# First head pair's bias tiles on GpSimd's queue, with two steps of the hand-over to attention in another order

## The chip, the cores and the metric

The kernel runs on 1 core of one Trainium2 chip. The metric is device time in microseconds (us), the median of several executions: 493.66 us over 3 runs before the change (493.31 to 494.21).

## The reference

Attention over 4 batches, 8 heads, 576 positions and head size 64, with a learned bias on relative position, and behind it a feed-forward block with a gate. All inputs and outputs are float32.

```python
scores = scale * np.matmul(q, k.transpose(0, 1, 3, 2))          # 4 x 8 x 576 x 576
x = (psi_rel / psi_i)[..., None]                                # log1p|i-j| / log1p(max(i,1))
h = np.maximum(x @ w1 + b1, 0.0)                                # 576 x 576 x 32
bias = h @ w2                                                   # 576 x 576 x 8, the same for every batch
attn = softmax(scores + bias)                                   # row maximum taken off first
x = matmul(attn, v)                                             # to 4 x 576 x 512
h = np.maximum(x @ w_in, 0.0)                                   # 4 x 576 x 1024
conv_out = sum over k of conv_w[k] * h[shifted by k - 1]
out = (h * sigmoid(conv_out)) @ w_out                           # 4 x 576 x 512
```

## The kernel before, in words

The program has three stages. The instructions of each engine run in the order in which the code emits them.

**The bias stage** computes the bias once for all batches. It goes over 36 blocks of 16 query rows (the loop over `i`). For a block, VectorE (DVE) and ScalarE (ACT) make the hidden layer (`y`, lines 246 and 250), TensorE (PE) contracts it with `w2` (line 267), and ACT copies the result from PSUM into one of five staging buffers (`st`, of which one is called `tl`, line 293). Each pair of blocks is then written to a scratch tensor in DRAM, `bias_d`, by one DMA of 607 KB on SyncE's (SP's) queue (line 306). This text calls blocks 2k and 2k+1 pair k, so pair 0 is the first.

**The bias tiles** are read back from `bias_d` by `load_bias(p, t)` (lines 173 to 184), a head pair p and a unit t at a time. The rows of queries are cut into five units: unit 0 has the first 64 rows of both heads on top of each other (one tile of 128 rows), units 1 to 4 have 128 rows each for each of the two heads. Each tile takes two DMAs, one for a head. Pair 0's tiles go through SP's queue, those of the other three head pairs through GpSimd's (POOL's) queue. A tile can be read once the pairs of blocks with its rows have landed in DRAM, and the queue that issues the read waits for that; whatever stands behind it on the same queue waits too. Unit 0's tile needs pairs 0 and 1, unit 1's needs pairs 2 to 5, and so on by four.

**The attention stage** walks over 16 combinations n of head pair and batch, and in each over the units t. For a unit, PE makes the scores (`s`, line 363), DVE adds the bias tile and takes the row extreme in one instruction per head (line 374, "reduce"), ACT takes the exponential with the row sum (line 388, "exponential") and marks the buffer by a two-column write (`sr`, line 342), PE transposes the result (lines 422 and 434), ACT and DVE copy the transposes from PSUM (lines 90 and 93), and PE multiplies them with V (line 471, "PV"). The transposes of line 422 go into free columns of the same PSUM tile as the last head's scores, so that head's reduce follows them. PV of a group (units 0 to 2, or 3 and 4) is cut into five parts, which wait in the queue `fill` and are put between other units' work. POOL stores and spreads the inverse row sums (lines 498 to 504) and applies them to the output (line 511).

Four units of n = 0, that is (0,0) to (0,3), start inside the bias loop, so that the stages overlap: at `i` = 13, 21, 29 and 34. Unit (0,3) has its scores and reduce there, its exponentials later. Behind the loop comes the **hand-over**: the last blocks are written, the tile of unit (0,4) is loaded, the first unit of n = 1 gets its scores, and the rest of `fill` is emitted. The list `flat` then sets the order of all units that are left. The main loop does, in iteration u, the scores and reduces of unit u+2, the exponentials of unit u+1, and the transposes of unit u, followed by parts of PV. `sums` says in which iteration the inverse row sums of the n before are transposed, `invert` (lines 486 and 487) makes them on DVE, and `load` and `load_v` fetch the next q, k and v through SP's queue.

**The feed-forward stage** takes the last 200 us and is not touched.

Of the kernel before, what the change touches and what calls it, by code (L numbers as in the profile page):

```python
# [19 lines left out]
def attention_ffn_kernel(  # L20
# [11 lines left out]
    nc = tc.nc  # L32
# [53 lines left out]
    NSEQ = len(seq)  # L86
# [50 lines left out]
    with tc.manual_schedule():  # L137
# [33 lines left out]
            nc.sync.dma_start(vt[TL:P, 9], v[b, p, TL:P, 4])  # L171

        def load_bias(p, t, cuts=()):
            queue = nc.gpsimd if p else nc.sync
            bt = bias_p.tile([P, 2, S], F32, name="bt") if t else bias0_p.tile([P, 1, S], F32, name="bt0")
            for a, e in zip((0,) + cuts, cuts + (P,)):
                for h in range(2):
                    c = (2 * p + h) * BW
                    if t:
                        i0 = TL + (t - 1) * P  # L180
                        queue.dma_start(bt[a:e, h], bias_rows[i0 + a:i0 + e, c:c + S])
                    else:
                        queue.dma_start(bt[TL * h:TL * h + TL, 0, :], bias_rows[0:TL, c:c + S])
            biast[p, t] = bt
# [155 lines left out]
        def turned_sp(n, t):  # L340
            tile = sp_p.tile([P, 2 * S + 2], F32R, name="sr", tag=spt[n, t][1])
            nc.scalar.activation(tile[:, 2 * S:], pars[:, 0:2], AF.Copy)
            spt[n, t] = (tile, None)


        def scores(n, t, h):
            p, b = seq[n]
            qt = qks[n]
            if h == 0:
                if n not in sms:  # L350
                    sms[n] = sm_p.tile([P, 9], F32, name="sm")
                nms[n, t] = sm_p.tile([P, 2], F32, name="nm")
                new_sp(n, t)
            ps = psum["s"].tile([P, 2, 512], F32, name="s")


            ops = [(h, h * QW + P * t, slice(0, P))] if t else [
                (hh, hh * (QW + TL), slice(TL * hh, TL * hh + TL)) for hh in range(2)
            ]
            for hh, qo, po in ops:  # L360
                for a in range(2):
                    rows = slice(D * a, D * a + D)
                    nc.tensor.matmul(  # L363
                        ps[po, a, 0:HS],
                        qt[rows, qo:qo + po.stop - po.start],
                        qt[rows, KO + hh * HS:KO + hh * HS + HS],
                        start=True,
                        stop=True,
                    )
            return ps  # L370

        def reduce(ps, n, t, h):
            bt = biast[seq[n][0], t]
            nc.vector.tensor_tensor_reduce(  # L374
                out=halves(spt[n, t][0][:, h]),
                in0=ps[:, :, 0:HS],
                in1=halves(bt[:, h]),
                op0=ALU.add,
                op1=ALU.min,
                scale=-scale,  # L380
                scalar=3.0e38,
                accum_out=nms[n, t][:, h:h + 1],
            )

        def expo(n, t, h):
            sp, nm = spt[n, t][0], nms[n, t]
            col = 4 * h + t - 1 if t else 8
            exps[n, t, h] = nc.scalar.activation(  # L388
                sp[:, h], sp[:, h], AF.Exp, bias=nm[:, h:h + 1], scale=-1.0,
                accum_out=sms[n][:, col:col + 1],  # L390
            )
# [187 lines left out]
        first = [(0, 0), (0, 1), (0, 2), (0, 3)]  # L579
        flat = [(n, t) for n in range(1, NSEQ) for t in units]  # L580
        flat.insert(0, (0, 3))
        flat.insert(3, (0, 4))
        NU = len(flat)

        def heads(t):
            return (0, 1) if t else (0,)

        fill = deque()
# [24 lines left out]
        for i in range(NBLK):  # L613
            nxt = bias_hidden(i + 1) if i + 1 < NBLK else None
            bias_mm(i, hidden)
            if last:
                bias_out(*last)
            last = (i,)
            hidden = nxt
            if i % 8 == 6 % 8 and i >= 6:  # L620
                load_bias(0, (i - 6) // 8)
            if i == 2:
                load(0)
            if i == 4:
                load_v(0)
            if i == 16:
                load(1)
            if i == 20:
                load_v(1)
            if i in starts:  # L630
                unit = unit_steps(*first[starts.index(i)])
            if unit:
                next(unit, None)
            for _ in range(max(0, i - starts[-1] + 1)):
                fill.popleft()()
        bias_out(*last)
        load_bias(0, 4, (96,))
        reduce(scores(*flat[1], 0), *flat[1], 0)
        while fill:
            fill.popleft()()  # L640
        early.close()
        psT = pool(ctx, "psT", 3, space=PSUM)
        psO = pool(ctx, "psO", 1, space=PSUM)
        psum.update(s=psS, tp=psT, o=psO)
        for h in heads(flat[0][1]):
            expo(*flat[0], h)
        turned_sp(*flat[0])
        pv_share = (2, 2, 1, 3, 2)
        hs_ff = {}
        raw_w = {}  # L650
# [4 lines left out]
        for u, (n, t) in enumerate(flat):  # L655
            p, b = seq[n]
            ui = units.index(t)
            sums = n - 1 if ui == 2 and n else None
            side = None
            if u + 2 < NU:  # L660
                for h in heads(flat[u + 2][1]):
                    if side is not None:
                        reduce(side, *flat[u + 2], 0)
                    side = scores(*flat[u + 2], h)
            if t:
                if side is None:
                    side = psS.tile([P, 2, 512], F32, name="s")
                side_transposes(side, n, t, sums)
            if u + 2 < NU:
                reduce(side, *flat[u + 2], h)  # L670
            if u + 1 < NU:
                for h in heads(flat[u + 1][1]):
                    expo(*flat[u + 1], h)
                turned_sp(*flat[u + 1])
            transposes(n, t, side, sums)
            next(job_steps, None)

            parts = len(fill) if u < 5 else pv_share[ui]
            while fill and parts > 0:
                fill.popleft()()  # L680
                parts -= 1
            next(job_steps, None)
            del spt[n, t]
            if u + 2 >= NU:
                f = u + 2 - NU
                hs_ff[0, f] = ffn_in(0, f)
            if u == 1 or n and ui == 2 and n + 2 < NSEQ:
                load(2 if u == 1 else n + 2)
            if u in conv_weights:
                conv_weights[u]()  # L690

            for at, do in ((u - 7, "load"), (u - 11, "split")):
                job = at // 2
                if at % 2 == 0 or not 0 <= job < 4 * KC + 2 * FE:
                    continue
                if job < 4 * KC:
                    src, dst = w_in[job // 4 * P:job // 4 * P + P], wi[job // 4]
                else:
                    src, dst = w_out[(job - 4 * KC) // 2 * P:(job - 4 * KC) // 2 * P + P], wo[(job - 4 * KC) // 2]
                cs = slice(job % 4 * 256, job % 4 * 256 + 256) if job < 4 * KC else slice(job % 2 * 256, job % 2 * 256 + 256)  # L700
                if do == "load":
                    raw_w[job] = (e_p if job % 3 else woe_p).tile([P, 256, 2], I32, name="raw_w", tag="h")
                    load_w(raw_w[job], src[:, cs])
                else:
                    job_steps = split_w_steps(e_p, dst[:, :, cs], raw_w.pop(job), ("cv", "cv"))
            if u + 2 < NU:
                n2, t2 = flat[u + 2]
                p2, b2 = seq[n2]
                if b2 == B - 1 and p2 + 1 < NP:
                    load_bias(p2 + 1, t2)  # L710
            if ui == (0 if n > 1 else 1) and n > 0:
                invert(n - 1)
            if ui == (2 if n > 1 else 3) and 1 <= n and n + 1 < NSEQ:
                load_v(n + 1)
            if ui == 3 and n > 0:
                store_sums(n - 1)
            if ui == 4 and n > 0:
                spread_sums(n - 1)
            if ends_group(n, t):
                fill.extend(pv_parts(n, t > 2))  # L720

            if ui == 2 and n > 1:
                apply_norm(n - 2)
            if n == NSEQ - 2 and ui > 1:
                x_parts(0, ui - 2)
            if n == NSEQ - 1 and ui == 0:
                x_parts(0, 3)
            if n == NSEQ - 1 and ui in (1, 2):
                load_wo(FE - 1 + ui)
# [209 lines left out]
```

## Time and profile before

| | |
|---|---|
| median of 3 runs | 493.66 us |
| the profiled execution | 493.83 us |
| its span, first to last instruction | 492.1 us |
| PE busy | 478.5 us (97%) |
| DVE busy | 376.9 us (77%) |
| ACT busy | 311.4 us (63%) |
| POOL busy | 154.0 us (31%) |
| granted TensorE clock | 1.00 throughout |

The span is that of one profiled execution; the difference to its device time, 1.7 us, lies around it. A share over the whole span says little here, since the three stages have different limits. So the rows further down are read by stage: the bias stage runs to about 62 us, the hand-over to about 78 us, attention to about 290 us. Idle time in the rows stands before the instruction that it precedes, with what released it.

### The profile page before, as it was taken

Reading aid. Unit: us, or ns where it says so; the run is one execution under the profiler, and the core shown is the slowest. Engines: PE = TensorE matmul, PEld = TensorE weight load, DVE = VectorE, ACT = ScalarE, POOL = GpSimd, SP = SyncE. Lnnn points to the kernel's source line nnn. Section 1 sums busy time; section 2 is a strip of 40 time slices with the busy share of each in tenths; the row PEclk is TensorE's granted clock in tenths of the full one; section 3 lists DMA queues with packets and bytes.
Section 4 is the critical chain, followed back from the end, with each engine's and each line's share of the span. In section 5 each row is a group of like instructions: output and inputs, shape, how many; then the busy total and the mean of one; then the engine's idle time right before and its main releaser. Section 6 shows DMA issues by size and latency. Waiting matters only on the chain.

```text
span 492.1 us, 11067 instructions
## 1 busy us (share of the span) xinstructions
PE 478.5 (97%) x4202; PEld 353.1 (72%) x4202; DVE 376.9 (77%) x871; ACT 311.4 (63%) x751; POOL 154.0 (31%) x215
## 2 busy tenths in 40 slices
PE   6989999999999999999999999999999999999996
PEld 4333356666666666666666689889988999899986
DVE  6989967788898889988898729944896279838930
ACT  6989877888888889888888736712542144224510
POOL 1000001245455735565547725160081005400000
PEclk9999999999999999999999999999999999999999
DMA  1999667388667895589751300002000300020011
GB/s 38 280 332 318 253 194 172 93 277 214 158 180 201 225 254 157 161 218 290 191 130 50 111 25 26 2 0 87 0 1 0 108 1 1 1 85 1 1 44 64
DMA packets 32584, 60.82 MB, mean 124 GB/s; under 512 B 7196, under 2 KB 15796, under 8 KB 32532
## 3 DMA queue, kind: packets, MB, share of 16 engines
q1 hardware_dynamic: 27380, 47.02, 33.2%
q0 software_dynamic: 4768, 12.77, 8.8%
q8 instruction: 33, 0.54, 0.5%
q10 hardware_dynamic: 384, 0.35, 0.2%
q14 instruction: 19, 0.16, 0.1%
HBM read 44.12 MB, written 15.98 MB: 122 GB/s over the span
## 4 chain that ended last, share of the span: by engine, by line
PE 88%; ACT 5%; DVE 3%; DMA 3%; issue 1%; SPq 0%; DVEq 0%
PE s L536 21%; PE o L471 17%; PE s L363 16%; PE tp L786 16%; PE tp L434 9%; PE o L786 4%; PE s L267 2%; DVE y L250 2%; DMA bias_d<-st 1%; ACT st L293 1%; ACT y L246 1%; ACT sp L388 1%; PE s L422 1%; DVE sp L374 1%; DMA pars<-in_par_dram 1%; DMA bt<-bias_d 1%
## 5 line engine op out<-in xcount | busy, mean ns | idle before, releaser
L374 DVE CUSTOM_DVE_ANT_0 sp<-s,bt 128x576 f32<-128x576 f32 x144 | 104.1, 754 | 32.3 <-PE s L363 13.1
L388 ACT ACTIVATE sp<-sp,nm 128x576 f32<-128x576 f32 x144 | 109.9, 767 | 0.8 <-DVE nm L374 0.8
L536 PEld LDWEIGHTS s<-xs,wi 128*128 128x128 f32 x768 | 102.8, 189 | 1.2 <-issue 0.5
L536 PE MATMUL s<-xs,wi 128*128 128x288 f32 x768 | 103.6, 296 | 0.0
L363 PE MATMUL s<-qk 64*128 64x288 f32 (+1 forms) x640 | 92.6, 431 | 0.5 <-DVE pty L93 0.2
L363 PEld LDWEIGHTS s<-qk 64*128 64x128 f32 (+1 forms) x640 | 46.9, 175 | 42.1 <-DVE nm L374 12.1
L786 PE MATMUL tp<-wo,g 128*128 128x512 f32 x288 | 70.7, 390 | 0.0
L434 PE MATMUL tp<-identr,sr 64*128 64x64 f32 x1184 | 64.3, 247 | 0.0
L786 PEld LDWEIGHTS tp<-wo,g 128*128 128x128 f32 x288 | 53.7, 188 | 11.8 <-DVE g L781 0.9
L434 PEld LDWEIGHTS tp<-identr,sr 64*128 64x128 f32 x1184 | 55.5, 136 | 5.6 <-issue 0.6
L761 DVE SCALAR_TENSOR_TENSOR cv<-h,cw,cv 128x575 f32<-128x575 f32 x64 | 55.2, 863 | 2.5 <-ACT cv L756 0.6
L548 ACT ACTIVATE h<-s 128x576 f32<-128x576 f32 x32 | 20.8, 651 | 55.2 <-PE s L536 55.2
L267 PE MATMUL s<-y,pars 128*32 128x512 f32 (+8 forms) x352 | 46.8, 513 | 4.0 <-DVE y L250 3.4
L250 DVE TENSOR_SCALAR y<-tl,inv,nb 128x576 f32<-128x576 f32 (+33 forms) x112 | 47.6, 506 | 0.1
L471 PE MATMUL o<-ptx,vt 128*64 128x320 f32 x300 | 47.0, 442 | 0.0
L471 PE MATMUL o<-pty,vt 128*64 128x256 f32 x320 | 44.2, 393 | 0.0
L133 POOL TENSOR_SCALAR xs<-x 128x576 fp32r<-128x576 f32 x16 | 15.2, 950 | 81.4 <-PE s L536 66.5
L267 PEld LDWEIGHTS s<-y,pars 128*32 128x32 f32 x352 | 17.3, 115 | 30.6 <-DVE y L250 15.3
L767 ACT ACTIVATE cv<-cv 128x576 f32<-128x576 f32 x32 | 21.8, 680 | 23.6 <-DVE cv L761 23.6
L498 POOL DMA_DIRECT2D r_d<-rt x16 | 10.0, 625 | 82.9 <-DVE rt L93 82.9
L768 DVE SCALAR_TENSOR_TENSOR cv<-cv,h 128x576 f32<-128x576 f32 x32 | 29.6, 924 | 5.7 <-ACT cv L767 5.7
L93 DVE COPY ptx<-tp 128x256 f32<-128x256 f32 (+1 forms) x64 | 32.0, 499 | 1.4 <-PE tp L434 1.2
(83 smaller groups left out, 635.8 us busy)
## 6 DMA issues: line engine op xcount, KB each, us to landing
qk<-in_qk_dram SPq DMA_DIRECT2D x32, 320.0 KB, 5.1
bias_d<-st SPq DMA_DIRECT2D x13, 607.0 KB, 5.0
bt<-bias_d POOLq DMA_DIRECT2D x24, 288.0 KB, 5.5
qk<-in_qk_dram SPq DMA_DIRECT2D x32, 144.0 KB, 5.4
rb<-r_d POOLq DMA_DIRECT2D x32, 144.0 KB, 3.1
vt<-in_v_dram SPq DMA_DIRECT2D x16, 256.0 KB, 5.9
raw_w<-in_moe_w_in_dram SPq DMA_DIRECT2D x16, 256.0 KB, 5.0
out_dram<-o SPq DMA_DIRECT2D x16, 256.0 KB, 2.0
```

The lines of the kernel that those rows point to most:

```text
L93: nc.vector.tensor_copy(o, i)
L250: nc.vector.tensor_scalar(y, dist[:, 0:n], inv[:, ig:ig + 1], nb1, op0=ALU.mult, op1=ALU.max)
L267: nc.tensor.matmul(ps[32 * j:32 * j + 32, a // 512 if n > 512 else blk % 2, 0:min(n - a, 512)], w2b, ys[j][:, a:min(n, a + 512)], start=Tr ...
L363: nc.tensor.matmul(ps[po, a, 0:HS], qt[rows, qo:qo + po.stop - po.start], qt[rows, KO + hh * HS:KO + hh * HS + HS], start=True, stop=True,)
L374: nc.vector.tensor_tensor_reduce(out=halves(spt[n, t][0][:, h]), in0=ps[:, :, 0:HS], in1=halves(bt[:, h]), op0=ALU.add, op1=ALU.min, scale ...
L388: exps[n, t, h] = nc.scalar.activation(sp[:, h], sp[:, h], AF.Exp, bias=nm[:, h:h + 1], scale=-1.0, accum_out=sms[n][:, col:col + 1],)
L434: tr = nc.tensor.transpose(ps[a][:, TL * s:TL * s + TL].bitcast(F32R), spf[ra, j:j + P], identr[ra, ra])
L471: nc.tensor.matmul(po[D * h:D * h + D, 0:width], vt[:, slot, :], pt[:, blk, :], start=(c == 0), stop=(c == 4),)
L536: nc.tensor.matmul(ps[:, a, 0:HS], wi[c][:, pw, cs], xss[b, c][:, px, a * HS:(a + 1) * HS], start=(i == 0), stop=(i == 3 * KC - 1),)
L761: nc.vector.scalar_tensor_tensor(out=cv[:, o:o + S - 1], in0=h[:, i:i + S - 1], scalar=cw[:, f, kk:kk + 1], in1=cv[:, o:o + S - 1], op0=AL ...
L768: nc.vector.scalar_tensor_tensor(out=cv, in0=cv, scalar=1.0, in1=h, op0=ALU.add, op1=ALU.mult)
L786: nc.tensor.matmul(ps, lhs(f, gi), wo[f][:, wj, cs], start=(f == 0 and i == 0), stop=(f == FC - 1 and i == 2),)
```

## The change

Pair 0's tiles for units 0 to 3 move from SP's queue to POOL's, and their loads are emitted two blocks earlier, right behind the last block that they need. Unit (0,4)'s tile stays on SP's queue. The exponentials of unit (0,3) are emitted ahead of the rest of `fill`. Unit (0,4) moves from fourth to fifth place in `flat`, and with it move the iterations for `sums` and `invert` of n = 0, the load of q and k for n = 2, and the place of one group of PV.

```diff
         def load_bias(p, t, cuts=()):
-            queue = nc.gpsimd if p else nc.sync
+            queue = nc.sync if cuts else nc.gpsimd
...
         flat.insert(0, (0, 3))
-        flat.insert(3, (0, 4))
+        flat.insert(4, (0, 4))
...
-            if i % 8 == 6 % 8 and i >= 6:
-                load_bias(0, (i - 6) // 8)
+            if i % 8 == 4:
+                load_bias(0, i // 8)
...
         load_bias(0, 4, (96,))
         reduce(scores(*flat[1], 0), *flat[1], 0)
+        for h in heads(flat[0][1]):
+            expo(*flat[0], h)
+        turned_sp(*flat[0])
         while fill:
             fill.popleft()()
         early.close()
         psT = pool(ctx, "psT", 3, space=PSUM)
         psO = pool(ctx, "psO", 1, space=PSUM)
         psum.update(s=psS, tp=psT, o=psO)
-        for h in heads(flat[0][1]):
-            expo(*flat[0], h)
-        turned_sp(*flat[0])
...
-            sums = n - 1 if ui == 2 and n else None
+            sums = n - 1 if ui == (2 if n > 1 else 3) and n else None
...
+            while fill and u == 5:
+                fill.popleft()()
             transposes(n, t, side, sums)
...
-            if u == 1 or n and ui == 2 and n + 2 < NSEQ:
-                load(2 if u == 1 else n + 2)
+            if u in (2, 4) or n > 1 and ui == 2 and n + 2 < NSEQ:
+                load(n + 2 if n > 1 else 2 + u // 4)
...
-            if ui == (0 if n > 1 else 1) and n > 0:
+            if ui == (0 if n > 1 else 2) and n > 0:
                 invert(n - 1)
```

SP's queue in the bias stage, with the reads of the bias tiles (`bt`) among the writes of the staging buffers; rows with a minus are of before.

```order
 L306 DMA bias_d<-st_125 128x2x607
-L183 DMA bt_266<-bias_d 64x576 x2
 L306 DMA bias_d<-st_132 128x2x607 x2
 L306 DMA bias_d<-tl 128x2x607
 L306 DMA bias_d<-st_124 128x2x607
-L181 DMA bt<-bias_d 128x576 x2
 L306 DMA bias_d<-st_125 128x2x607
```

The reads leave SP's queue here and at two later places. On POOL's queue they stand between its first fills of constants and the first inverse row sums (`r_d`).

```order
 L318 MEMSET rr_155 128x128
 L222 MEMSET kv 128x2
+L183 DMA bt_243<-bias_d 64x576 x2
+L181 DMA bt<-bias_d 128x576 x6
 L498 DMA r_d<-rt 2x4x128
 L499 DMA r_d<-rt 2x1x64
```

Nothing else of POOL stands between the eight reads. ACT at the hand-over, before the change: the last copies of the bias stage (`st`), the copy of an output of PV (`x`), then the exponentials.

```order
L293 ACTIVATE st_125<-s,kv 128x576
L293 ACTIVATE st_125<-s,kv 128x31
L90 ACTIVATE x_121<-tp 128x320
L388 ACTIVATE sp,sm<-sp,nm 128x576 x2
L342 ACTIVATE sr<-pars 128x2
L388 ACTIVATE sp,sm<-sp,nm 128x576
```

And after it.

```order
L293 ACTIVATE st_125<-s,kv 128x576
L293 ACTIVATE st_125<-s,kv 128x31
L388 ACTIVATE sp,sm<-sp,nm 128x576 x2
L342 ACTIVATE sr<-pars 128x2
L90 ACTIVATE x_121<-tp 128x320
L388 ACTIVATE sp,sm<-sp,nm 128x576
```

The two exponentials of unit (0,3) and the write behind them have moved ahead of the copy. PE in iterations 4 to 6 of the main loop, before: scores (L363), transposes (L422, L434), transposes of the inverse row sums (L426) and PV (L471).

```order
L363 MATMUL s<-qk 128x288 x4
L422 MATMUL s<-identr,sr 128x64 x2
L426 MATMUL s<-ident,rr_154 128x64 x2
L434 MATMUL tp<-identr,sr 128x64 x16
L471 MATMUL o<-pty,vt_106 64x256 x10
L363 MATMUL s<-qk 64x288 x4
L422 MATMUL s<-identr,sr 128x64 x2
L434 MATMUL tp<-identr,sr 128x64 x16
L471 MATMUL o<-ptx,vt_107 64x320 x6
L363 MATMUL s<-qk 128x288 x4
L422 MATMUL s<-identr,sr 128x64 x2
L434 MATMUL tp<-identr,sr 128x64 x16
```

And after it.

```order
L363 MATMUL s<-qk 128x288 x4
L422 MATMUL s<-identr,sr 128x64 x2
L434 MATMUL tp<-identr,sr 128x64 x16
L471 MATMUL o<-ptx,vt_107 64x320 x10
L363 MATMUL s<-qk 64x288 x4
L422 MATMUL s<-identr,sr 128x64 x2
L426 MATMUL s<-ident,rr_154 128x64 x2
L471 MATMUL o<-pty,vt_106 64x256 x10
L434 MATMUL tp<-identr,sr 128x64 x16
L363 MATMUL s<-qk 128x288 x4
L422 MATMUL s<-identr,sr 128x64 x2
L434 MATMUL tp<-identr,sr 128x64 x16
```

The wider group of PV (`ptx`, of n = 1) comes first and whole, the other one (`pty`, of n = 0) one iteration later and ahead of that iteration's transposes; the sums move with it.

## Rows read from the trace of the kernel before

**Rows 1.** Busy us by stretch (PE, PEld, DVE, ACT, POOL), granted clock, DMA share, GB/s.
```profile
26.00:62.00 36.00, 33.50 (x270) 12.39 (x270) 33.73 (x84) 31.55 (x59) 0.00 (x0) 1.00 0.87 296
...
78.00:285.00 207.00, 207.00 (x2368) 137.91 (x2365) 174.94 (x498) 169.40 (x472) 109.44 (x168) 1.00 0.68 182
```
**Rows 2.** Chain of waits, bias stage: start us, us, what.
```profile
14.64 7.12 DMA bias_d<-st
...
22.32 3.31 DMA bt<-bias_d
```
**Rows 3.** Timeline of VectorE: start us, us, engine line op, [idle before <-releaser].
```profile
25.80 0.76 DVE L374 CUSTOM_DVE_ANT_0 sp<-s,bt 128x576 f32<-128x576 f32 x1 [0.99 <-PE s L267]
...
44.72 5.71 DVE L250 TENSOR_SCALAR y<-tl,inv,nb 128x436 f32<-128x436 f32 x13
...
66.77 0.76 DVE L374 CUSTOM_DVE_ANT_0 sp<-s,bt 128x576 f32<-128x576 f32 x1 [1.23 <-ACT x L90]
...
68.30 0.76 DVE L374 CUSTOM_DVE_ANT_0 sp<-s,bt 128x576 f32<-128x576 f32 x1 [0.77 <-PE s L422]
```
**Rows 4.** Timeline of TensorE, same columns.
```profile
27.00 1.86 PE L267 MATMUL s<-y,pars 128*32 128x352 f32 x8 [1.48 <-DVE y L250]
...
68.01 0.25 PE L422 MATMUL s<-identr,sr 64*128 64x64 f32 x2 [0.90 <-ACT sp L388]
...
79.78 0.72 PE L363 MATMUL s<-qk 64*64 64x288 f32 x8
```
**Rows 5.** Chain of waits at the hand-over.
```profile
66.45 1.52 ACT sp L388 x4
...
74.07 0.09 DVE rr L486
...
74.19 0.22 DVE rr L487
...
76.05 0.72 PE s L363 x3
...
77.54 2.31 PE o L471 x20
```
**Rows 6.** Timeline of ScalarE, bias stage and hand-over.
```profile
18.06 1.45 ACT L293 ACTIVATE st<-s,kv 128x960 f32<-128x960 f32 x2
...
66.01 0.44 ACT L90 ACTIVATE x<-tp 128x320 f32<-128x320 f32 x1 [2.88 <-PE tp L471]
```
**Rows 7.** Timeline of SyncE's queue: issues of DMAs.
```profile
21.82 1.09 SPq L183 DMA_DIRECT2D bt<-bias_d  x2
23.00 1.05 SPq L306 DMA_DIRECT2D bias_d<-st  x2
...
72.03 0.62 SPq L154 DMA_DIRECT2D qk<-in_qk_dram  x1
```
**Rows 8.** Timeline of GpSimd: its first DMAs.
```profile
79.31 0.54 POOL L499 DMA_DIRECT2D r_d<-rt  x1
84.18 1.07 POOL L504 DMA_DIRECT2D rb<-r_d  x2 [4.33 <-DMA r_d<-rt]
```
**Rows 9.** DMA issues near 79, 84 and 96 us: count, KB each, us to landing.
```profile
r_d<-rt POOLq DMA_DIRECT2D x1, 0.5 KB, 4.3
...
rb<-r_d POOLq DMA_DIRECT2D x2, 144.0 KB, 3.1
...
bt<-bias_d POOLq DMA_DIRECT2D x2, 144.0 KB, 4.9
```
**Rows 10.** Timeline of GpSimd and VectorE, near 105 and 139 us.
```profile
104.67 1.69 POOL L181 DMA_DIRECT2D bt<-bias_d  x3
...
105.96 0.28 DVE L99 TENSOR_SCALAR wu<-raw_w 128x256 int32<-128x256 int32 x1
...
139.16 1.52 POOL L511 TENSOR_TENSOR x<-x,rb 128x576 f32<-128x576 f32 x1
...
139.29 1.53 DVE L99 TENSOR_SCALAR wu<-raw_w 128x256 int32<-128x256 int32 x1
```

## Prediction

> **What bounds the kernel now.** The page was read first, then busy time by stretch, then the chain of waits through the first 82 us, then the timelines of the engines that it passes. From 78 us to 285 us PE is busy in all of its 207.00 us [rows 1]: attention runs at PE's pace, and whatever comes late before 78 us comes late at the end. So the question is how much earlier or later PE gets into its unbroken stretch, which begins with PV at 77.54 [rows 5].
>
> In the bias stage no engine is free to catch up. DVE is busy 33.73 of 36.00 us, PE 33.50, ACT 31.55 [rows 1], and they hand blocks to each other. The chain enters this stage through a transfer: pair 1's write is issued at 14.64 and takes 7.12 us, so it lands at 21.76; the second half of unit 0's tile is issued at 22.32 and lands 3.31 us later, at 25.63 [rows 2]. DVE, which runs in order, has by then been idle 0.99 us ahead of unit 0's reduce at 25.80 [rows 3]; behind it PE waits 1.48 us for the next `y` [rows 4]. The release that the row of DVE names is an older one of PE; the chain shows the tile. I found no wait in the stretch behind it that would take up a further delay: what DVE, PE and ACT do next all hangs on that reduce or on the `y` behind it. So each 1 us by which unit 0's tile is later counts as 1 us at the end.
>
> At the hand-over the chain goes through ACT: it copies PV's output at 66.01 after 2.88 us of idleness [rows 6], and then makes four pieces of exponentials in 1.52 us from 66.45 [rows 5], two for unit (0,3). PE waits 0.90 us for them, up to 68.01 [rows 4], and DVE's second reduce of unit (1,1) follows at 68.30, since its PSUM tile is also written by those transposes [rows 3]. From there DVE has no idle row until PV has begun, and DVE's last copy lets PE go on at 76.05 [rows 5].
>
> **The exponentials.** They need only the reduces of unit (0,3), done while ACT sits idle ahead of 66.01. Two of them with their write fit into those 2.88 us. PE's wait goes, and the reduce at 68.30 can follow the one at 66.77, which takes 0.76 [rows 3]: it starts at 67.53, 0.8 us sooner. That is all that can go there, because the reduce at 66.77 waits for scores that PE makes after PV, in an order that stays. What is late next is DVE, which then runs without a break up to the end of the hand-over, so the 0.8 us arrives whole at PV. ACT is not late: it got rid of 1.52 us and of the write ahead of DVE's stretch.
>
> **The unit put later.** Iterations 0 to 4 hold the same units as before in another order, so PE, ACT and DVE have the same work ahead of PV, with one exception. `invert` took DVE 0.09 + 0.22 = 0.31 us of the chain [rows 5], ahead of the reduces and of the copy that frees PSUM for PE. One iteration later it stands behind the last copy that PE waits for. That is another 0.3 us. The transposes of the sums move behind that point too; they are 0.1 us at most. Behind PV's start the order of PV changes, not its amount, and PE has always something to do: five parts of the wide group, then five of the narrow one, then an iteration without PV, in which DVE and ACT have two iterations of PV as a lead. I cost this at nothing; if the cover failed, an iteration without PV would cost the 0.2 us or so by which a reduce follows PE's scores. The load for n = 2 is issued an iteration later; before, its last issue is at 72.03 [rows 7] and its first use at 79.78 [rows 4], 7.75 us later. One iteration less, some 2 us, leaves more than the 4.9 us that the slowest transfer in rows 9 takes. SP has nothing urgent behind it. POOL's first inverse sums come an iteration later, with DMAs and a multiplication behind them that nobody in attention waits for.
>
> Sum of these two edits: 0.8 + 0.3 = 1.1 us sooner.
>
> **The tiles on POOL's queue.** Eight reads leave SP's queue. What they held up was writes: pairs 3 and 4 were issued from 23.00 [rows 7], though pair 3's copy was done at 18.06 + 1.45 = 19.51 [rows 6]. Nobody waited for these writes, so their release gains nothing. The two earlier blocks of program order gain nothing either, since the read of unit 0's tile already started the moment pair 1 had landed: 21.82 [rows 7] against 21.76. What counts is how long the read takes from there on another queue. POOL answers later than SP: its second DMA is issued at 79.31 and lands 4.3 us later [rows 8, 9], at 83.61, and the read that waits for it starts at 84.18 [rows 8], 0.57 us after, where SP took 0.06. So the first half starts at 21.76 + 0.57 = 22.33 and the second, half of 1.07 us later [rows 8], at 22.87. A transfer of 144 KB from POOL then takes 3.1 us with little beside it and 4.9 us beside loads of q, k and v [rows 9]: landing at 25.97 or at 27.77 in place of 25.63, that is 0.3 or 2.1 us later. I take the middle, 1.2 us: pair 3 has mostly gone by then, but pair 4, which used to start behind the read, now moves beside it. Below nothing, at most the 0.99 us of DVE's idleness can go.
>
> The tiles of units 1 to 3 are hidden. Unit 2's reduce follows DVE's chain of `y` from 44.72 to 50.43 without idle time [rows 3], so its tile lay ready; a later landing by 1 or 2 us, with DVE itself 1 us later, stays covered. Without that cover each would cost like unit 0's.
>
> Sum: 1.2 - 1.1 = 0.1 us later. From the profiled execution's own 493.83 us that gives 493.9; that execution lies 0.17 us over the median of the runs, so the forecast on the median's scale is 493.8 us. Its own range, with 0.3 and 2.1 for the tile: 492.9 to 494.7.
>
> **Rivals.** First, slower: GpSimd is kept from making its transfers while DVE runs its `y` chains. The two engines do exclude each other in some operations: DVE's tensor-scalar takes 0.28 us beside POOL's DMA issues near 105 us, but 1.53 us beside a POOL multiplication that ends at 140.68, and ends right after that [rows 10]. `y` is a tensor-scalar from SBUF to SBUF as well, and these run back to back. If POOL must wait until DVE stops, unit 0's tile is started when DVE runs dry, at 25.80 - 0.99 = 24.81; the second half is issued at 25.35 and lands at 28.45, 2.7 us later than the reduce starts now. On the median: 493.66 - 1.1 + 2.7 = 495.3 us. Unit 2's tile would then wait for 50.43 too and cost 3.1 us more, and the other two as much at most: 504.5 us as the worst. It decides against the kernel from a delay of 2.1 us on. Against it: POOL's DMA issues keep their length beside the tensor-scalar, three in 1.69 us [rows 10]; but none of them stood beside a chain of such operations, so the trace does not settle it. The Trainium skill states this rule (SBUF — State Buffer, section "SBUF: two separate sides"): DMAs issued from GpSimd get no descriptors written while VectorE holds the ports that they share. By that rule the time is this rival's; the 1.53 us row agrees that there is a lock, and no run here shows it for a chain of DMAs.
>
> Second, faster: the tile is no later than now, because POOL's queue holds nothing else and is served beside SP's, up to the whole 0.99 us of idleness. Then only the gain stands: 492.6 us, at best 491.6. For it: POOL's quiet 3.1 us; against it: 0.57 us of a slower answer, and SP's queue had nothing ahead of the read.
>
> Third: the hand-over gives back its gain. The later unit or the bunched PV makes PE wait once more by about the 0.8 us won, and the tile's 1.2 us stands: 494.6 us. Against it: PE's full 207 us [rows 1].
>
> **How the numbers follow.** A measurement of this kernel tells about 0.2%, 1.0 us, from no change. Forecast 0.46, nearly all within it; first rival 0.24, slower; second 0.18, faster; third 0.12, half of it slower. Some of the forecast's own spread goes over each edge. That gives faster 0.20, same 0.46, slower 0.34. The range of 8 in 10 reaches from 492.2, most of the second rival, to 496.5, most of the first with one tile late.
>
> **What would show it.** In the profile after, unit 0's reduce should start near 27.0 rather than 25.80, with some 2 us of idleness ahead of it; PE should show no wait for exponentials at the hand-over; PV should begin 9.7 us after the first reduce of unit (1,1) starts (now 66.77 to 77.54, 10.8 us). Idle rows of DVE ahead of the reduces of units 1 to 3 would speak for the first rival; a reduce before 25.80 for the second; any idle time of PE behind PV's start for the third. The forecast is wrong if the tile's read takes under 2.9 us or over 5 us on POOL's queue.

## The result and the profile after

| | us, median (lowest to highest) | runs |
|---|---|---|
| before | 493.38 (492.94 to 494.21) | 6 |
| after | 497.51 (497.16 to 498.15) | 6 |

The ratio is 1.0082, 95% interval 1.0071 to 1.0093: slower by 4.1 us, or 0.8%, and clear of the noise. The profiled execution of after took 497.35 us with a span of 495.6 us. The forecast was 493.8 us, range 492.2 to 496.5.

The first view is the timeline of GpSimd after: start us, us, instruction, and in brackets the idle time ahead. The first row holds the first of the two reads of unit 0's tile alone; the second is the pair of reads for unit 1.

```profile
21.77 3.00 POOL L183 DMA_DIRECT2D bt<-bias_d  x1 [19.34 <-DMA vt<-in_v_dram]
...
29.24 1.09 POOL L181 DMA_DIRECT2D bt<-bias_d  x2 [3.94 <-DMA bias_d<-tl]
```

One issue took 3.00 us; a pair takes 1.09 us elsewhere. So the second half of the tile was issued at 21.77 + 3.00 = 24.77. What else ends there is in VectorE's timeline after, same columns:

```profile
10.58 14.07 DVE L250 TENSOR_SCALAR y<-tl,inv,nb 128x512 f32<-128x512 f32 x34
24.62 0.11 DVE L336 MEMSET sp<- 128x64 f32 x1
...
29.42 0.76 DVE L374 CUSTOM_DVE_ANT_0 sp<-s,bt 128x576 f32<-128x576 f32 x1 [4.61 <-DMA bt<-bias_d]
...
33.89 0.67 DVE L93 COPY ptx<-tp 128x256 f32<-128x256 f32 x2 [1.20 <-PE tp L434]
...
54.89 0.76 DVE L374 CUSTOM_DVE_ANT_0 sp<-s,bt 128x576 f32<-128x576 f32 x1
...
71.22 0.76 DVE L374 CUSTOM_DVE_ANT_0 sp<-s,bt 128x576 f32<-128x576 f32 x1 [1.22 <-ACT x L90]
...
71.91 0.75 DVE L374 CUSTOM_DVE_ANT_0 sp<-s,bt 128x576 f32<-128x576 f32 x1
...
79.74 0.17 DVE L486 TENSOR_SCALAR rr<-sm 128x9 f32<-128x9 f32 x1
```

VectorE's chain of `y`, a row of tensor-scalars without idle time (34 of them in this view), ends at 10.58 + 14.07 = 24.65, and GpSimd's issue ends 0.12 us behind it. The issue stood beside the last 3 us of the row, some eight operations of 0.4 us. Unit 0's reduce then waits 4.61 us for the tile and starts at 29.42 in place of 25.80 [rows 3]: 3.62 us later. Unit 2's reduce at 54.89 has no idle time ahead of it, as before. At the hand-over the reduce at 71.91 follows the one at 71.22 directly; the 0.77 us of [rows 3] are gone.

Rows of DMA issues after (count, KB each, median us from issue to landing): both halves of the tile, the first half alone, and pair 1's write:

```profile
bt<-bias_d POOLq DMA_DIRECT2D x2, 144.0 KB, 5.0
...
bt<-bias_d POOLq DMA_DIRECT2D x1, 144.0 KB, 5.5
...
bias_d<-st SPq DMA_DIRECT2D x1, 607.0 KB, 6.7
```

Pair 1 landed near 14.53 + 6.7 = 21.2, and GpSimd began its read some 0.6 us after. The two halves of the tile took 5.5 and 4.5 us (median 5.0) from issue to landing. The 5.5 hold the 3.00 us of the first issue itself; what the reduce waited for is the second half, up to 29.25, where SP's second took 3.31 [rows 2]. SP meanwhile was free of the reads. The row below holds its writes of pairs 2, 3 and 4, all issued by 22.30, where before those of pairs 3 and 4 went out from 23.00 on [rows 7] (timeline of SP after):

```profile
18.83 3.47 SPq L306 DMA_DIRECT2D bias_d<-st  x3
```

The timeline of TensorE after, and its busy time by stretch (the columns are those of [rows 1]; the granted clock comes third from the end, 1.00 is 2.4 GHz and 0.5 is 1.2 GHz):

```profile
30.61 2.46 PE L267 MATMUL s<-y,pars 128*32 128x352 f32 x8 [5.12 <-DVE y L250]
33.00 0.83 PE L434 MATMUL tp<-identr,sr 64*128 64x64 f32 x10
...
71.18 0.41 PE L422 MATMUL s<-identr,sr 64*128 64x64 f32 x2
...
80.74 2.91 PE L471 MATMUL o<-ptx,vt 128*64 128x320 f32 x20
```
```profile
28.00:30.00 2.00, 0.00 (x0) 0.00 (x0) 0.58 (x1) 0.00 (x0) 0.76 (x2) 1.00 0.97 378
30.00:32.00 2.00, 1.39 (x7) 0.72 (x8) 2.00 (x8) 1.50 (x4) 0.33 (x1) 0.62 0.70 207
32.00:34.00 2.00, 2.00 (x19) 0.88 (x18) 0.81 (x3) 0.14 (x1) 0.00 (x0) 0.53 0.24 92
34.00:36.00 2.00, 1.45 (x14) 0.42 (x8) 1.95 (x7) 2.00 (x5) 0.00 (x0) 1.00 0.00 0
82.00:289.00 207.00, 206.87 (x2373) 137.96 (x2369) 173.92 (x497) 169.01 (x471) 109.13 (x168) 1.00 0.67 182
```

PE stood 5.12 us, and then its clock was at the lower level for most of 30 to 34 us (0.62 and 0.53 in these rows): the same eight matmuls took 2.46 us in place of 1.86 [rows 4]. VectorE's `ptx` copy behind them waits 1.20 us and starts at 33.89. The same row of the kernel before is this:

```profile
29.43 0.67 DVE L93 COPY ptx<-tp 128x256 f32<-128x256 f32 x2 [0.35 <-PE tp L434]
```

The copy is thus 4.46 us later, 0.84 more than the reduce. From there all of the bias stage is shifted by about that much. At the hand-over PE's 0.90 us of [rows 4] are gone (71.18 has no idle time), and PE is again busy in 206.87 of 207 us from 82 us on. The chain of waits after gives PV's start (start us, us, what):

```profile
80.81 2.84 PE o L471 x20
```

So PV starts 80.81 - 77.54 [rows 5] = 3.27 us later: 4.46 lost in the bias stage, 1.19 won at the hand-over. The two profiled executions differ by 3.52 us, so 0.25 us arise elsewhere; that part is open. The medians differ by 4.13: the 0.61 us between lie in how each profiled execution stands to its median (0.45 above before, 0.16 below after).

### The profile page after: what moved, and what is told of

It reads as the page before. It is cut to its first block, busy times and chain, and to the rows that moved or that the text cites. A ratio compares the mean times of both kernels' runs of the same rounds, so it can differ in the third digit from the quotient of the medians.

```text
span 495.6 us, 11065 instructions
## 1 busy us (share of the span) xinstructions
PE 479.1 (97%) x4202; PEld 353.1 (71%) x4202; DVE 376.2 (76%) x871; ACT 311.5 (63%) x751; POOL 160.3 (32%) x223
## 4 chain that ended last, share of the span: by engine, by line
PE 84%; DVE 0%; issue 0%; DVEq 0%
PE s L536 21%; PE o L471 17%; PE s L363 16%; PE tp L788 16%; PE tp L434 9%; PE o L788 4%; PE s L422 1%; PE s L426 0%; DVE pty L93 0%; DVE sp L374 0%; DVE o L796 0%; PE tp L491 0%; DVE ptx L93 0%; PE tp L565 0%; DVEq L796 0%
## 5 line engine op out<-in xcount | busy, mean ns | idle before, releaser
L363 PE MATMUL s<-qk 64*128 64x288 f32 (+1 forms) x640 | 93.0, 431 | 0.7 <-DVE ptx L93 0.2
L363 PEld LDWEIGHTS s<-qk 64*128 64x128 f32 (+1 forms) x640 | 46.8, 175 | 41.8 <-DVE nm L374 12.5
L434 PE MATMUL tp<-identr,sr 64*128 64x64 f32 x1184 | 64.6, 248 | 0.0
L434 PEld LDWEIGHTS tp<-identr,sr 64*128 64x128 f32 x1184 | 55.8, 136 | 6.7 <-issue 1.5
L471 PE MATMUL o<-ptx,vt 128*64 128x320 f32 x300 | 46.8, 442 | 0.0
L471 PE MATMUL o<-pty,vt 128*64 128x256 f32 x320 | 44.2, 393 | 0.0
L90 ACT ACTIVATE ptx<-tp 128x256 f32<-128x256 f32 (+1 forms) x64 | 26.3, 437 | 7.6 <-PE tp L434 7.2
```

The costliest lines, as they stand in the source:

```text
L363: nc.tensor.matmul(ps[po, a, 0:HS], qt[rows, qo:qo + po.stop - po.start], qt[rows, KO + hh * HS:KO + hh * HS + HS], start=True, stop=True,)
L434: tr = nc.tensor.transpose(ps[a][:, TL * s:TL * s + TL].bitcast(F32R), spf[ra, j:j + P], identr[ra, ra])
L471: nc.tensor.matmul(po[D * h:D * h + D, 0:width], vt[:, slot, :], pt[:, blk, :], start=(c == 0), stop=(c == 4),)
```

## The experiments

Three theories were tested. A: GpSimd's issue of the read cannot proceed while VectorE runs its chain of `y`. B: the read is late because the writes that SP now sends earlier share its transfer engines. C: the edits at the hand-over lose the time. Each ratio is to the kernel before on the same chip.

**The tiles alone.** The kernel before with only the two edits on the tiles:

```diff
-            queue = nc.gpsimd if p else nc.sync
+            queue = nc.sync if cuts else nc.gpsimd
...
-            if i % 8 == 6 % 8 and i >= 6:
-                load_bias(0, (i - 6) // 8)
+            if i % 8 == 4:
+                load_bias(0, i // 8)
```

> The kernel before with only the four tiles moved to GpSimd's queue. Theory A (GpSimd's first DMA issue is shut out while VectorE runs its chain of y, and the hand-over edits gain 1.2 us): 493.4 + 4.5 = 497.9 us, with unit 0's reduce at 29.4 us and a first issue of 3 us on GpSimd. Theory C (the hand-over edits lose, the tiles cost little): 493 to 495 us.

Measured: 498.31 us, ratio 1.0087 (1.0071 to 1.0103). Its timelines of GpSimd, VectorE and TensorE:

```profile
21.80 3.00 POOL L183 DMA_DIRECT2D bt<-bias_d  x1 [19.38 <-DMA vt<-in_v_dram]
...
13.76 10.93 DVE L250 TENSOR_SCALAR y<-tl,inv,nb 128x476 f32<-128x476 f32 x27
...
29.54 0.76 DVE L374 CUSTOM_DVE_ANT_0 sp<-s,bt 128x576 f32<-128x576 f32 x1 [4.71 <-DMA bt<-bias_d]
...
82.02 2.38 PE L471 MATMUL o<-pty,vt 128*64 128x256 f32 x20
```

The long issue and the late reduce are there without the other edits. The first issue again takes 3.00 us and ends, at 24.80, 0.1 us behind the row of tensor-scalars (13.76 + 10.93 = 24.69). In the timeline of the kernel before, PV stands here:

```profile
77.47 2.38 PE L471 MATMUL o<-pty,vt 128*64 128x256 f32 x20
```

So PV starts 4.55 us later. The whole loss is the tiles'.

**The hand-over alone.** After, with those two edits undone:

```diff
-            queue = nc.sync if cuts else nc.gpsimd
+            queue = nc.gpsimd if p else nc.sync
...
-            if i % 8 == 4:
-                load_bias(0, i // 8)
+            if i % 8 == 6 % 8 and i >= 6:
+                load_bias(0, (i - 6) // 8)
```

> The changed kernel with all of pair 0's tiles back on SyncE's queue at their old places. Theory A: 493.4 - 1.2 = 492.2 us, no wait of TensorE for exponentials, PV from 76.4 us. Theory C: 496 us or more.

Measured: 492.16 us, ratio 0.9972 (0.996 to 0.9983). From its timelines of VectorE and TensorE:

```profile
25.49 0.76 DVE L374 CUSTOM_DVE_ANT_0 sp<-s,bt 128x576 f32<-128x576 f32 x1 [0.52 <-DMA bt<-bias_d]
...
75.97 2.91 PE L471 MATMUL o<-ptx,vt 128*64 128x320 f32 x20
```

PV starts 1.50 us sooner than at 77.47; 0.31 of that is the reduce's start at 25.49 in place of 25.80, the other 1.19 the hand-over, as in after. C falls: these edits win 1.2 us by the medians (493.37 to 492.16).

**Only unit 0's tile back on SP.** After, with the other three tiles left on GpSimd:

```diff
-            queue = nc.sync if cuts else nc.gpsimd
+            queue = nc.gpsimd if p or 0 < t < 4 else nc.sync
...
-            if i % 8 == 4:
+            if i == 6:
+                load_bias(0, 0)
+            if i % 8 == 4 and i > 4:
                 load_bias(0, i // 8)
```

> The changed kernel with only unit 0's tile back on SyncE's queue; units 1 to 3 stay on GpSimd's. Theory A, in which the other three reads meet gaps in VectorE's chains: 492.2 to 492.6 us. If GpSimd's queue as such were the cost, each of the three tiles would still cost some of it: 493.5 to 496 us.

Measured: 492.37 us, ratio 0.9972 (0.9963 to 0.9982), as with all tiles on SP. The timelines of VectorE and of GpSimd:

```profile
25.38 0.76 DVE L374 CUSTOM_DVE_ANT_0 sp<-s,bt 128x576 f32<-128x576 f32 x1 [0.39 <-DMA bt<-bias_d]
...
29.70 6.54 DVE L250 TENSOR_SCALAR y<-tl,inv,nb 128x304 f32<-128x304 f32 x18
...
44.30 5.73 DVE L250 TENSOR_SCALAR y<-tl,inv,nb 128x436 f32<-128x436 f32 x13
...
53.22 4.40 DVE L250 TENSOR_SCALAR y<-tl,inv,nb 128x544 f32<-128x544 f32 x9
```
```profile
30.61 1.38 POOL L181 DMA_DIRECT2D bt<-bias_d  x2 [28.19 <-DMA bias_d<-tl]
44.95 1.26 POOL L181 DMA_DIRECT2D bt<-bias_d  x2 [12.96 <-DMA vt<-in_v_dram]
54.02 1.35 POOL L181 DMA_DIRECT2D bt<-bias_d  x2 [7.81 <-DMA bias_d<-st]
```

Unit 0's tile alone costs the whole time. The issues for units 1 to 3 take 1.26 to 1.38 us a pair, a little more than the 1.07 us of [rows 8], and cost nothing that shows. The first of them is GpSimd's first transfer in this kernel, so being the first is not what makes an issue long.

The time is the forecast one, but not for the reason given: these issues met no gaps. Each pair went out inside a row of tensor-scalars that has neither idle time nor another operation in it. The pair at 30.61 was through at 31.99, and the row around it ran on to 36.24. So GpSimd can get a turn between back-to-back tensor-scalars, and theory A does not hold for every chain. One difference is that these pairs were issued 0.7 to 0.9 us into their rows, and unit 0's read in after at least 11 us into its own (21.77 against 10.58). No run tests whether that is what decides.

**Gaps in VectorE's chain.** After, with a copy of 128x128 from PSUM behind each of four blocks of `y`; nothing uses its result:

```diff
+        gap = {}
...
+            if blk in (11, 12, 13, 14):
+                nc.vector.tensor_copy(gap["o"], gap["i"][:, 0:P])
...
+        gap["i"] = psB.tile([P, 512], F32, name="tp")
+        gap["o"] = bias_c.tile([P, P], F32, name="gap")
+        nc.tensor.transpose(gap["i"][:, 0:P], ident, ident)
```

> The changed kernel with four copies of 128x128 from PSUM on VectorE, one behind each of blocks 11 to 14 of y, as gaps for GpSimd; the copies' result is used by nobody. Theory A: GpSimd's first issue shrinks from 3.0 to 1.3 us or less, unit 0's reduce comes 1.5 to 2 us sooner than 29.4, total 494.8 to 496.2 us. Theory B (the tile is late because writes of pairs 3 and 4 now run beside it): the issue stays at 3 us, and the copies add up to 1 us: 497.5 to 498.5 us.

Measured: 495.39 us, ratio 1.0037 (1.0023 to 1.005). Its timelines of GpSimd (both issues, then the second alone), VectorE and TensorE, and the clock by stretch:

```profile
22.07 1.35 POOL L183 DMA_DIRECT2D bt<-bias_d  x2 [19.66 <-DMA bias_d<-st]
...
22.77 0.66 POOL L183 DMA_DIRECT2D bt<-bias_d  x1
```
```profile
21.11 1.25 DVE L252 TENSOR_SCALAR y<-tl,inv,nb 128x384 f32<-128x384 f32 x3
22.27 0.28 DVE L257 COPY gap<-tp 128x128 f32<-128x128 f32 x1
22.47 1.22 DVE L252 TENSOR_SCALAR y<-tl,inv,nb 128x368 f32<-128x368 f32 x3
23.60 0.29 DVE L257 COPY gap<-tp 128x128 f32<-128x128 f32 x1
...
27.63 0.76 DVE L378 CUSTOM_DVE_ANT_0 sp<-s,bt 128x576 f32<-128x576 f32 x1 [1.92 <-DMA bt<-bias_d]
```
```profile
28.82 2.47 PE L271 MATMUL s<-y,pars 128*32 128x352 f32 x8 [2.62 <-DVE y L252]
```
```profile
30.00:32.00 2.00, 2.00 (x20) 0.80 (x17) 0.91 (x3) 0.00 (x0) 1.03 (x2) 0.50 0.43 108
```

This is the run that shows A for unit 0's read. No edit touches GpSimd, SP or the transfers; VectorE has more to do; and yet both issues took 1.35 us in place of 3.54, the reduce starts at 27.63, 1.79 us sooner than in after, and the median falls by 2.1 us. The first issue had a copy beside it (22.27). The second had none: it passed from 22.77 to 23.43, beside tensor-scalars alone, soon after that copy. The reduce is still 1.83 us later than in [rows 3], since the read's landing stays slow (next but one), and PE's clock fell here too, after 2.62 us of idle time.

**PE kept busy.** After, with 20 matmuls of 128x512 (two records each in the trace) behind block 14, whose results nobody reads:

```diff
+            if i == 14:
+                idle = psB.tile([P, 512], F32, name="tp")
+                for _ in range(5):
+                    for j in range(4):
+                        nc.tensor.matmul(
+                            idle[32 * j:32 * j + 32, 0:512], w2b, dist[:, 0:512], start=True, stop=True
+                        )
```

> The changed kernel with 20 matmuls of 128x512 on TensorE behind block 14, whose result nobody uses, to fill its 5 us of idleness while VectorE waits for unit 0's tile. If the granted clock's fall to 0.5 after that idleness is worth 0.85 us: clock 1.00 from 30 to 34 us, first transposes 0.85 us sooner, 496.7 us. If that 0.85 us comes from something else (the wake-up of the chain): 497.5 us, or later if the matmuls run past the tile's landing.

Measured: 497.12 us, ratio 1.0068 (1.0049 to 1.0086). Its timelines of TensorE and VectorE, and the clock by stretch:

```profile
25.34 4.52 PE L620 MATMUL tp<-tl,pars 128*32 128x512 f32 x40
30.24 1.86 PE L267 MATMUL s<-y,pars 128*32 128x352 f32 x8 [0.38 <-DVE y L250]
```
```profile
29.05 0.76 DVE L374 CUSTOM_DVE_ANT_0 sp<-s,bt 128x576 f32<-128x576 f32 x1 [4.16 <-DMA bt<-bias_d]
...
32.68 0.67 DVE L93 COPY ptx<-tp 128x256 f32<-128x256 f32 x2 [0.35 <-PE tp L434]
```
```profile
30.00:32.00 2.00, 1.76 (x8) 0.55 (x8) 2.00 (x7) 1.34 (x4) 0.00 (x0) 1.00 0.86 276
32.00:34.00 2.00, 1.42 (x20) 0.76 (x20) 1.60 (x5) 1.36 (x4) 0.00 (x0) 1.00 0.08 20
```

The clock stays at 2.4 GHz, the eight matmuls take 1.86 us again, and reduce and `ptx` copy are both 3.25 us later than before: nothing is lost between them. In the trace the clock's part is thus 0.84 us, as read above. By the medians it is 0.4 us with overlapping intervals, so the size at the end of the kernel is not settled by this run.

**A write beside the read.** After, with unit 0's tile on SP, but behind pair 3's write, and the other tiles on GpSimd:

```diff
-            queue = nc.sync if cuts else nc.gpsimd
+            queue = nc.gpsimd if p or 0 < t < 4 else nc.sync
...
-            if i % 8 == 4:
+            if i == 8:
+                load_bias(0, 0)
+            if i % 8 == 4 and i > 4:
                 load_bias(0, i // 8)
```

> The changed kernel with unit 0's tile on SyncE's queue, but behind pair 3's write, which then runs beside the read; units 1 to 3 on GpSimd's queue. Theory A (sharing the transfer engines costs little): unit 0's reduce at 25.8 to 26.8 us, 492.3 to 493.3 us. Theory B (a write beside the read is what made the tile late): reduce at 27.5 us or later, 494 us or more.

Measured: 493.05 us, ratio 0.9994 (0.9982 to 1.0006). The DMA issues of that read, and VectorE's timeline:

```profile
bt<-bias_d SPq DMA_DIRECT2D x2, 144.0 KB, 4.0
```
```profile
25.84 0.76 DVE L374 CUSTOM_DVE_ANT_0 sp<-s,bt 128x576 f32<-128x576 f32 x1 [1.02 <-DMA bt<-bias_d]
```

With one more write on its way, SP's read takes 4.0 us, the median of its halves, where that of the kernel before takes 3.1 by the same view. By the medians that costs some 0.7 us against the run with the tile ahead of the write (492.37, on another chip). B as the main cause falls; as a second term of about 1 us in the read it stands.

**The exponentials alone.** Before, with only the exponentials moved:

```diff
+        for h in heads(flat[0][1]):
+            expo(*flat[0], h)
+        turned_sp(*flat[0])
         while fill:
...
-        for h in heads(flat[0][1]):
-            expo(*flat[0], h)
-        turned_sp(*flat[0])
         pv_share = (2, 2, 1, 3, 2)
```

> The kernel before with only the exponentials of unit (0,3) moved ahead of fill. By the prediction's split (0.8 us here, 0.3 us from the unit put later): 492.6 us. If unit (0,4)'s tile, used an iteration sooner than in the changed order, is late for it: 493 us or more.

Measured: 492.69 us, ratio 0.9981 (0.9969 to 0.9993): 0.75 us gained. The hand-over with both edits gained 1.21, so the unit put later has 0.46; the intervals of the two runs overlap, and only the first part is shown by itself.

**The write first.** The hand-over alone (all tiles on SP), with the loads of n = 0 moved behind pair 1's write:

```diff
-            if i == 2:
-                load(0)
             if i == 4:
+                load(0)
+            if i == 8:
                 load_v(0)
```

> The hand-over edits alone, all tiles on SyncE's queue, and the loads of q, k and v for n = 0 two to four blocks later, so that pair 1's write is issued ahead of them. If the 7 us until pair 1 lands are the four loads ahead of it: it lands by 19 us, unit 0's tile by 24.7 us, VectorE's 0.99 us of idleness goes, 491.2 us. If they are not: 492.2 us as without it, or later if q and k for n = 0 are late for the scores at 24.1 us.

Measured: 492.23 us, ratio 0.9971 (0.9961 to 0.9981), no better than the hand-over alone. VectorE's timeline shows the intended effect, a reduce without idle time:

```profile
24.92 0.76 DVE L374 CUSTOM_DVE_ANT_0 sp<-s,bt 128x576 f32<-128x576 f32 x1
```

Its profiled execution starts PV at 75.39, 0.58 us sooner than that of the hand-over alone, but the medians do not differ. The expected gain of 1 us had counted on 0.99 us of idle time, of which the hand-over's kernel has only 0.52 in its trace; where the rest went is open.

Three versions beat both kernels, at 0.997 of before: the hand-over alone, with unit 0's tile on SP, and with the write first. The runs do not tell them apart.

## Why the prediction was wrong

**The bound.** Right. PE is busy behind PV's start, before (207.00 of 207 us) and after (206.87), and what was late at unit 0's reduce was late at PV.

**The step that failed** is in the part on the tiles: "So the first half starts at 21.76 + 0.57 = 22.33 and the second, half of 1.07 us later [rows 8], at 22.87." GpSimd's answer was sized well (some 0.6 us; pair 1 landed 0.6 us sooner, so the read began at 21.77). The issue itself was not: 3.00 us, not 0.54, so the second half went out at 24.77, 1.90 us later than forecast. The 1.07 us came from a stretch of attention where VectorE runs reduces and copies; here VectorE ran tensor-scalars back to back up to 24.65. The experiment with gaps, which changes VectorE's work alone, shows that this row of operations held the issue. Why GpSimd got no turn between them stays open: in the run with only unit 0's tile on SP it got one inside three other rows. Set against SP's read in [rows 2], the loss adds up: the second half is issued at 24.77 and not at 22.32 (2.45 us), and takes 4.48 us to land and not 3.31 (1.17 us): 3.62 us, as the reduce shows. The sum had 1.2, and its upper bound of 2.1 took the issue's length as certain.

The landing was bounded by 3.1 and 4.9 us, and the second half's 4.48 lies inside. The first half's 5.5 lies outside, and over the 5 us named as a sign, because it holds the long issue. The reason given for a slow landing, a write that moves beside the read, is borne out by the run behind pair 3's write: 4.0 us on SP's queue. Whether GpSimd's queue adds to it is not shown.

**A term that was missing.** With 3.6 us of delay PE stands for 5.12 us, its clock falls, and the stage loses 0.84 us more. The sum had only delays that pass through one to one.

**The first rival** had the right mechanism for unit 0. It let the first issue begin when VectorE ran dry, at 24.81, and the second at 25.35; in fact the first ended there and the second went out at 24.77. Its price was short all the same, 2.7 us where 3.62 came, because it took a landing in quiet (3.1 us), and it lacked the clock's 0.84. It had a chance of 0.24; the row against it, DMA issues that kept their length beside one tensor-scalar [rows 10], stood beside a single operation and could not speak for a chain, as the text itself said. The Trainium skill (SBUF — State Buffer, section "SBUF: two separate sides") states the lock, and that such a DMA waits until VectorE's operation ends and about 0.1 us more; the trace agrees on the 0.1 us, with 0.12 us from the chain's end to the end of the issue. What the page says is about one operation; here the issue waited through some eight, and in other chains it did not have to.

**Units 1 to 3.** Right: hidden, as unit 2's reduce without idle time and the run with only unit 0's tile on SP show. The rival's worst case of 504.5 us, with every tile held by its chain, did not come; inside chains those pairs were issued in 1.26 to 1.38 us. Idle time ahead of these reduces was named as the sign of the first rival. It stayed away, although that rival was right for unit 0.

**The hand-over.** Right: forecast 1.1 us, 1.19 in the trace of after, 1.21 by the medians of the hand-over alone. Of its two parts only the exponentials' 0.75 us (forecast 0.8) is shown by itself. The cover for the unit put later held (PE 206.87 of 207 us). The second and third rival fall: the tile was not as early as on SP, and nothing was given back.

## What to carry to other kernels

A transfer on the path is at risk when GpSimd issues it while VectorE runs SBUF-to-SBUF tensor-scalars back to back: the issue can last until the end of VectorE's chain, as here, or pass with 0.2 to 0.3 us more a pair, as for units 1 to 3. Until it is known which, let the range hold the end of the chain, and not only the issue's length elsewhere in the kernel. When one row of the trace speaks for a cover and it comes from another neighbourhood, the range has to hold the case without it, and whatever that case does to the writes beside it and to PE's clock. A change of several edits is worth splitting: here 1.2 us of gain lay under 4.9 us of loss (498.31 against 493.37).

## What the runs showed of the hardware

- In after and with the tiles alone, GpSimd's issue beside some eight back-to-back tensor-scalars of 0.4 us took 3.00 us and ended 0.1 us behind the last of them. With copies from PSUM of 0.28 us in that chain two issues took 1.35 us. With only unit 0's tile on SP, pairs issued 0.7 to 0.9 us into other such chains took 1.26 to 1.38 us with no gap in them.
- The clock fell to 1.2 GHz after PE had stood 5.12 us, and also in the run with gaps, where it had stood 2.62 us; behind the 1.48 us of [rows 4] it stayed at 1.00 [rows 1]. With the 20 matmuls in the break it did not fall.
- The halves of the tile (144 KB) took 3.1 us in the median on SP's queue in the kernel before, and 4.0 us with one more write of 607 KB ahead of them. On GpSimd's queue in after, the half whose issue was not held took 4.5 us beside such writes.
